# Retention decay moved from x into q, with the opening and the last tile of a fused retention + MLP kernel reordered

## The chip, the cores and the metric

The kernel runs on one core of a Trainium2 chip. The core has five engines that run at the same time, each through its own list of instructions in order: TensorE (PE, matrix products; its weight loads are shown apart as PEld), VectorE (DVE), ScalarE (ACT), GpSimd (POOL) and SyncE (SP). They wait for each other through semaphores. Sixteen DMA engines move data between the main memory and the core's SBUF; SP, ACT and POOL issue the transfers. TensorE writes to eight banks of PSUM, and only DVE and ACT read them in this kernel.

The metric is the device time of one execution in microseconds, lower is better. Three runs of the kernel before took 316.67, 316.84 and 317.51 us; the median is 316.84.

## What is computed

Eight batches of retention (attention without softmax, with a decay by distance), and after it an MLP over all 4608 tokens with the activation h * cos(h):

```python
def _attn_ref(q, k, v) -> np.ndarray:      # 8 batches, 8 heads, 576 positions, 64 wide
    B, H, S, D_ = q.shape
    scale = 1.0 / np.sqrt(D_)
    scores = scale * np.matmul(q, k.transpose(0, 1, 3, 2))
    gamma = 1.0 - 2.0 ** (-5.0 - np.arange(H, dtype=np.float32))
    pos = np.arange(S)
    rel = pos[:, None] - pos[None, :]
    Dmat = np.where(rel >= 0, gamma[:, None, None] ** rel[None, :, :], 0.0)
    ret = scores * Dmat[None, :, :, :]
    return np.matmul(ret, v).astype(np.float32)

def _moe_ref(x, w_in, w_out) -> np.ndarray:   # w_in 512 x 2048, w_out 2048 x 512
    h = x @ w_in
    g = h * np.cos(h)
    return (g @ w_out).astype(np.float32)
```

The decay gamma^(i-j) is split into two factors: gamma^i / 8 belongs to the query's position (the 8 is the scale), gamma^-j to that of k and v. So a causal mask of zeros and ones is all that the scores need, and a running state (the sum of k times v over the chunks so far) carries what earlier chunks give.

## The kernel before

**Retention.** A batch has 576 positions, cut into four chunks of 128 and one of 64 (`ck_of`). For a chunk r the steps are:
- k is cast to bf16 into `kqb` (`cast`, L314), v is multiplied by gamma^-j into `vb` (`vmul`, L305), both on POOL.
- k and q are needed with the head dimension on the partitions, in `kqt`. Batches 2 to 7 are turned by a DMA transpose (`prep`, L321). Batches 0 and 1 are turned on TensorE against the identity: `turn_k` (L352), and `turn_q` (L369), which turns a pair of heads for all positions; an eviction on ACT or DVE copies the PSUM bank into `kqt`. Batch 0's q is loaded in four pieces (`load_q0`) and cast by DVE (`cast_q0`, L278).
- `scores` (L405) multiplies q and k for the eight heads, and DVE applies the causal mask (`mk`) into `rt`, in two instructions.
- `rest` (L433) multiplies the state `sb` by q and `rt` by vb into one bank, adds the chunk's part to the state bank `st`, copies it into `sb` with two ACT instructions, and multiplies the result by `up` (gamma^i / 8) on DVE into `xt` (L476). `xt` is the MLP's input, x turned.

`up` is made by four exponentials on ACT in the opening (`consts_b`, L243), gamma^-j (`wv`) by eight small ones.

**MLP.** Nine blocks of 512 tokens. `mlp1` (L489) makes 128 of the 2048 hidden columns: four matmuls, the cosine on ACT (as a sine, `cb`), the product on DVE (`gt`). `mlp2` (L514) makes a quarter of a tile of 128 output tokens: four matmuls against `wout`; after the fourth quarter ACT copies the bank into `osb` and a store is issued by ACT. Block 0 goes through its 16 steps quarter by quarter over the four tiles (step n is tile n % 4, quarter n // 4), so step 4 first needs the second quarter of w_out, step 8 the third, step 12 the fourth. Later blocks go tile by tile. The retention of batch j+1 is put in between the steps of block j by hand.

**The order is written out by hand** in `emit` (L550). Each engine does its work in the order in which it is emitted there, and so do the queues of SP and POOL. What bears on the change:
- SP loads k0, the four pieces of q, then v0, k1, v1, k2, k3, v2, v3, k4, v4 of batch 0, without waits. After it come the ten loads of k and v of batch 1, whose first waits for w_out's first quarter (`after=[w]`).
- POOL makes the casts and multiplies of batch 0, and between them issues the loads of w_in in five pieces (hidden tiles 0-1, 2-3, 4-7, 8-11, 12-15, `WI`), after the ones of chunk 4 those of w_out in four pieces, with q of batch 1 (`load_qx`) after the second. These transfers convert from float32 to bf16 on the way.
- TensorE turns and processes chunks 0 to 3 of batch 0, with `spin` (products of the identity with itself, whose results nobody reads) in the pauses. Then the 16 steps of `mlp1` of block 0 with chunk 4's turn, scores and rest after steps 2, 4 and 6; then the 16 steps of `mlp2` of block 0, with batch 1's turns, scores and rest after steps 7 to 14. The turn of batch 1's chunk 2 uses the bank `po`, as `rest` does.
- Between `exp` and the sine ACT loads another table (L604), in the list after the eviction of k3's turn.
- The last output tile is made like any other: 16 matmuls of 512 columns, one copy, one store.

## Time and profile before

| what | us |
|---|---|
| profiled execution, whole | 316.4 |
| its span | 314.7 |
| median of three runs | 316.84 |
| TensorE busy | 303.5 |
| DVE busy | 174.1 |
| ACT busy | 162.3 |
| POOL busy | 93.1 |
| multiply into `xt`, 128x512, on DVE, 31 times | 0.69 each |
| cast of k or q, 128x512, on POOL, 56 times | 0.61 each |
| multiply of v, 128x512, on POOL, 32 times | 1.04 each |
| cast of q, 128x576, on DVE, 4 times | 0.46 each |
| eviction of a turned q, 128x576: ACT / DVE | 0.65 / 0.75 |
| cast or eviction of k's turn, 128x512: ACT / DVE | 0.59 / 0.68 |

The profile is that of one execution; the times of all runs scatter around it, so it is read by its own span, and the 1.7 us between span and time are what lies around the program. Busy shares are averages: in the opening, up to about 20 us, TensorE waits for loads and for other engines; from there on it is nearly always at work. The page's strips over 40 slices of the span show the same, with the rate of the DMA engines under them:

```profile
PE   6989999999999999999999999999999999999996
POOL 2692027535454434453445424210000000000000
DMA  7999999999999999999999999940001100120021
```

Each digit is a slice of 7.9 us, in tenths. The DMA engines are busy without a pause from the second slice to the 26th.

### The profile page before, as it was taken

To read this page: it belongs to the slowest core of one execution; us is meant where nothing else is said; L and a number is where in the kernel's file an instruction comes from. 1 tells how busy PE (TensorE), PEld (TensorE's weight loads), DVE (VectorE), ACT (ScalarE), POOL (GpSimd) and SP (SyncE) were. 2 spreads that over 40 slices of the span, in tenths; PEclk is the share of its full clock that TensorE was granted. 3 is DMA by queue.
4 is the path that set the end of the run, shared out by engine and by line. 5 is a ranking of instruction groups with operands and counts; after the bars stand their busy time and mean duration, and the time that the engine had idled before them with its cause. 6 is when DMAs were issued, how large, how long until landed. Compare 5 with 4: busy or idle time off the path is not lost.

```text
span 314.7 us, 6424 instructions
## 1 busy us (share of the span) xinstructions
PE 303.5 (96%) x2516; PEld 159.6 (51%) x2552; DVE 174.1 (55%) x301; ACT 162.3 (52%) x290; POOL 93.1 (30%) x128
## 2 busy tenths in 40 slices
PE   6989999999999999999999999999999999999996
PEld 5754455666544455445544554455444544444442
DVE  3567624787527743685458644765387438405700
ACT  7566525785337533763277236723473257316711
POOL 2692027535454434453445424210000000000000
PEclk9999999999999999999999999999999999999999
DMA  7999999999999999999999999940001100120021
GB/s 218 213 168 204 203 220 247 264 192 209 212 256 183 217 210 247 217 224 217 259 208 202 225 204 221 172 85 35 33 0 38 66 33 0 42 94 1 12 83 74
DMA packets 142814, 48.85 MB, mean 155 GB/s; under 512 B 132544, under 2 KB 137664, under 8 KB 142784
## 3 DMA queue, kind: packets, MB, share of 16 engines
q1 hardware_dynamic: 132320, 34.22, 59.7%
q0 software_dynamic: 5280, 4.78, 9.5%
q10 hardware_dynamic: 5184, 9.44, 8.9%
q8 instruction: 20, 0.33, 0.4%
q14 instruction: 10, 0.08, 0.1%
HBM read 36.70 MB, written 9.44 MB: 147 GB/s over the span
## 4 chain that ended last, share of the span: by engine, by line
PE 90%; DMA 2%; DVE 2%; ACT 2%; issue 2%; SPq 1%; POOL 0%; DVEq 0%
PE mm L401 59%; PE mm L403 20%; PE po L401 6%; PE sc L401 4%; DMA kn<-in_k_dram 2%; PE st L401 1%; DVE gt L507 1%; DVE rt L428 1%; SPq L276 1%; ACT sb L471 0%; DVE xt L476 0%; ACT L604 0%; ACT osb L538 0%; ACT kqt L365 0%; SPq L267 0%
## 5 line engine op out<-in xcount | busy, mean ns | idle before, releaser
L507 DVE TENSOR_TENSOR gt<-mm,cb 128x512 bf16<-128x512 f32 (+2 forms) x160 | 101.1, 637 | 66.2 <-ACT cb L504 63.6
L401 PE MATMUL mm<-xt,win 128*128 128x512 bf16 (+2 forms) x468 | 116.0, 358 | 1.0 <-DVE xt L476 0.3
L504 ACT ACTIVATE cb<-mm,c_pih 128x512 bf16<-128x512 f32 (+2 forms) x160 | 101.9, 645 | 27.8 <-PE mm L403 27.0
L401 PE MATMUL mm<-wout,gt 128*128 128x512 bf16 x408 | 111.8, 380 | 2.3 <-issue 1.7
L401 PEld LDWEIGHTS mm<-xt,win 128*128 128x128 bf16 x480 | 44.6, 98 | 48.8 <-DVE gt L507 2.3
L401 PEld LDWEIGHTS mm<-wout,gt 128*128 128x128 bf16 x432 | 39.3, 98 | 45.1
L403 PE MATMUL mm<-xt,win 128*128 128x512 bf16 (+2 forms) x160 | 57.2, 358 | 0.3
L538 ACT ACTIVATE osb<-mm 128x512 f32<-128x512 f32 x36 | 21.5, 597 | 68.0 <-PE mm L403 68.0
L403 PE MATMUL mm<-wout,gt 128*128 128x512 bf16 x144 | 54.6, 379 | 0.5
L308 POOL TENSOR_TENSOR vb<-vn,wv 128x512 bf16<-128x512 f32 (+1 forms) x40 | 41.7, 1043 | 29.2 <-DMA vn<-in_v_dram 24.7
L428 DVE TENSOR_TENSOR rt<-sc,mk 128x512 bf16<-128x512 f32 (+1 forms) x78 | 45.8, 625 | 4.8 <-PE sc L403 4.8
L476 DVE TENSOR_TENSOR xt<-po,up 128x512 bf16<-128x512 f32 (+1 forms) x39 | 24.7, 634 | 41.9 <-PE po L403 41.8
L471 ACT ACTIVATE sb<-st 64x256 bf16<-64x256 f32 x64 | 24.2, 378 | 40.1 <-PE st L403 38.7
L318 POOL CAST kqb<-kn 128x512 bf16<-128x512 f32 (+1 forms) x40 | 24.4, 611 | 65.2 <-DMA kn<-in_k_dram 56.2
L318 POOL CAST kqb<-qn 128x512 bf16<-128x512 f32 (+1 forms) x30 | 18.5, 615 | 17.7 <-DMA qn<-in_q_dram 17.5
L403 PEld LDWEIGHTS mm<-xt,win 128*128 128x128 bf16 x160 | 15.7, 98 | 15.7
L403 PEld LDWEIGHTS mm<-wout,gt 128*128 128x128 bf16 x144 | 14.1, 98 | 17.0
L401 PE MATMUL po<-rt,vb 128*64 128x128 bf16 (+1 forms) x273 | 15.2, 220 | 0.0
L401 PE MATMUL sc<-kqt 64*128 64x128 bf16 (+1 forms) x273 | 14.7, 215 | 0.0
L401 PEld LDWEIGHTS po<-kqt,sb 128*128 128x128 bf16 x124 | 8.6, 98 | 7.8 <-DVE rt L428 1.6
L401 PEld LDWEIGHTS po<-rt,vb 128*64 128x64 bf16 (+1 forms) x273 | 9.3, 108 | 5.9 <-DVE rt L428 2.1
L401 PE MATMUL po<-kqt,sb 128*128 128x128 bf16 (+1 forms) x124 | 11.2, 213 | 0.4 <-DVE rt L428 0.2
(88 smaller groups left out, 133.2 us busy)
## 6 DMA issues: line engine op xcount, KB each, us to landing
out_dram<-osb ACTq DMA_DIRECT2D x36, 256.0 KB, 3.3
kn<-in_k_dram SPq DMA_DIRECT2D x32, 256.0 KB, 4.7
vn<-in_v_dram SPq DMA_DIRECT2D x32, 256.0 KB, 5.3
qn<-in_q_dram SPq DMA_DIRECT2D x24, 256.0 KB, 4.8
wout<-in_moe_w_out_dram POOLq DMA_DIRECT2D x4, 512.0 KB, 14.5
win<-in_moe_w_in_dram POOLq DMA_DIRECT2D x3, 512.0 KB, 8.2
qn<-in_q_dram SPq DMA_DIRECT2D x4, 288.0 KB, 4.7
kn<-in_k_dram SPq DMA_DIRECT2D x8, 128.0 KB, 3.5
```

Source lines behind the costliest of these rows:

```text
L276: s.dma("sp", f"q0_{c}", lambda e: e.dma_start(dst, src), writes=[self.bQN[c]])
L308: self.s.op(eng, lambda e: e.tensor_tensor(bass.AP(self.VB[i][r], 0, v3), self.staged("v", r, v3[1:]), bass.AP(self.WV, r * H_, [[NCH * H_ ...
L318: self.s.op(eng, lambda e: e.tensor_copy(o, f), reads=[self.bST32[x][r]], writes=[bt[i][r]])
L401: self.nc.tensor.matmul(o, a, b, **kw)
L403: return s.done("pe", self.nc.tensor.matmul(o, a, b, **kw), reads, writes)
L428: self.s.op("dve", lambda e: e.tensor_tensor(bass.AP(self.RT[k][hp], 0, p3), bass.AP(sc[0], 0, p3), bass.AP(self.MK, 0, [[CH, ck], [0, NP] ...
L471: s.op("act", lambda e: e.activation(bass.AP(self.SB[r % 2], 64 * hp * 512 + 64 * hp, [[512, 64], [128, NP], [1, D_]]), bass.AP(self.ST, 6 ...
L476: s.op("dve", lambda e: e.tensor_tensor(bass.AP(self.XT, t0, [[NP * XR, 128], [XR, NP], [1, ck]]), bass.AP(po, 0, [[512, 128], [CH, NP], [ ...
L504: s.op("act", lambda e: e.activation(co, mo, AF.Sin, bias=self.C_PIH.ap(), scale=1.0), reads=[bm, self.bC], writes=[bcb])
L507: s.op("dve", lambda e: e.tensor_tensor(bass.AP(g, dt * TB + o, [[16 * TB, 128], [1, n]]), mo, co, ALU.mult), reads=[bm, bcb], writes=[bg])
L538: s.op("act", lambda e: e.activation(o.ap(), m.ap(), AF.Copy), reads=[bm], writes=[bo])
```

## The change

- **Decay.** `xt` becomes a plain copy. q is multiplied by gamma^i / 8 instead: for batches 0 and 1 in `turn_q`'s eviction, now always on DVE, and for the others on POOL in `qmul`, which replaces the cast of q and uses a new small table `upn` made by eight exponentials on ACT (`consts_n`).
- **Batch 0's casts.** q's casts move from DVE to POOL; k3's cast moves from POOL to ACT. The copies into `xt` of chunks 1 and 2 go to ACT, and scores and rest of chunks 1 and 3 use other banks.
- **Loads.** k1 comes before v0 and k2 before v1. k4 and v4 wait for the first piece of w_in, the loads of batch 1 for the last one. w_in has four equal pieces. The first is issued after v1's multiply, the other three after v3's.
- **Order.** Chunk 4 of batch 0 moves from after steps 2, 4, 6 to after steps 6, 8, 10 of `mlp1`. Batch 1's turns, scores and rest in `mlp2` of block 0 move by one step or two, and the turn of chunk 2 takes another bank. The sine's table load comes after chunk 2's rest.
- **Last tile.** The new function `last` makes it in two halves of 256 columns; DVE and ACT copy one each, SP and ACT store one each.

```diff
-WI = (0, 2, 4, 8, 12, 16)
+WI = (0, 4, 8, 12, 16)
...
+    def consts_n(self):
+        s = self.s
+        for h in range(H_):
+            s.op("act", lambda e: e.activation(
+                bass.AP(self.UPN, h, [[NCH * H_, 128], [H_, NCH]]), self.IP.ap(), AF.Exp,
+                bias=self.C_LN8.ap(), scale=self.lng[h]), reads=[self.bIP, self.bC], writes=[Buf()])
+        self.bUPN.w = [Tok("act", "act", s.count["act"], {})]
...
     def cast_q0(self, c):
         n = 9 * D_
-        self.s.op("dve", lambda e: e.tensor_copy(
+        self.s.op("pool", lambda e: e.tensor_copy(
...
+    def qmul(self, eng, b, r):
+        i = b % 2
+        self.mul(eng, "q", r, self.KQB[i][r], DM, 2 * DM, self.UPN, self.bUPN, self.bQB[i][r])
+
+    def mul(self, eng, x, r, t, o, pitch, w, bw, bt):
+        ck = ck_of(r)
+        self.s.op(eng, lambda e: e.tensor_tensor(
+            bass.AP(t, o, [[pitch, ck], [D_, H_], [1, D_]]),
+            self.staged(x, r, [[D_, H_], [1, D_]]),
+            bass.AP(w, r * H_, [[NCH * H_, ck], [1, H_], [0, D_]]), ALU.mult),
+            reads=[self.bST32[x][r], bw], writes=[bt])
...
     def prep(self, b, r):
-        for x in "kq":
-            self.cast("pool", x, b, r)
+        self.cast("pool", b, r)
+        self.qmul("pool", b, r)
         self.vmul("pool", b, r)
...
-        fn = (lambda e: e.activation(o, f, AF.Copy)) if eng == "act" else (lambda e: e.tensor_copy(o, f))
-        done = s.op(eng, fn, reads=[bm], writes=[Buf()])
+        u = bass.AP(self.UP, c * S_, [[NP * S_, 128], [9, 64], [1, 9]])
+        done = s.op("dve", lambda e: e.tensor_tensor(o, f, u, ALU.mult), reads=[bm, self.bUP],
+                    writes=[Buf()])
...
-        s.op("dve", lambda e: e.tensor_tensor(
-            bass.AP(self.XT, t0, [[NP * XR, 128], [XR, NP], [1, ck]]),
-            bass.AP(po, 0, [[512, 128], [CH, NP], [1, ck]]),
-            bass.AP(self.UP, q0, [[NP * S_, 128], [S_, NP], [1, ck]]), ALU.mult),
-            reads=[bpo, self.bUP], writes=self.bXT[t0 // GR:(t0 + ck) // GR])
+        o = bass.AP(self.XT, t0, [[NP * XR, 128], [XR, NP], [1, ck]])
+        f = bass.AP(po, 0, [[512, 128], [CH, NP], [1, ck]])
+        fn = (lambda e: e.activation(o, f, AF.Copy)) if eng == "act" else (lambda e: e.tensor_copy(o, f))
+        s.op(eng, fn, reads=[bpo], writes=self.bXT[t0 // GR:(t0 + ck) // GR])
...
+    def last(self, j, st):
+        s, g, n = self.s, self.GT[j % 2], DM // 2
+        i = self.n_osb % self.NOSB
+        for half in range(2):
+            m, bm = self.bank()
+            self.group([(m[:, 0:n],
+                         bass.AP(g, c * TB + 128 * st, [[16 * TB, 128], [1, 128]]),
+                         bass.AP(self.WOUT, c * DM + n * half, [[16 * DM, 128], [1, n]]),
+                         dict(start=c == 0, stop=c == 15)) for c in range(16)],
+                       self.bGT[j % 2] + self.bWOUT, [bm])
+            o, f = self.OSB[i][:, n * half:n * half + n], m[:, 0:n]
+            b = Buf()
+            b.w, b.r = list(self.bOSB[i].w), list(self.bOSB[i].r)
+            if half:
+                s.op("act", lambda e: e.activation(o, f, AF.Copy), reads=[bm], writes=[b])
+            else:
+                s.op("dve", lambda e: e.tensor_copy(o, f), reads=[bm], writes=[b])
+            dst = bass.AP(self.out, (TB * j + 128 * st) * DM + n * half, [[DM, 128], [1, n]])
+            s.dma(("sp", "act")[half], f"o_{half}", lambda e: e.dma_start(dst, o), reads=[b])
```

The order in `emit`, new lines only (the old order is that described above):

```python
        self.load("k", 0, 0)
        self.load_q0()
        for x, r in (("k", 1), ("v", 0), ("k", 2), ("v", 1), ("k", 3), ("v", 2), ("v", 3)):
            self.load(x, 0, r)
        self.consts_a()
        for c in range(NP):
            self.consts_b(c)
        self.consts_n()
        self.cast("pool", 0, 0)
        for c in range(NP):
            self.cast_q0(c)
        self.cast("pool", 0, 1)
        self.vmul("pool", 0, 0)
        self.cast("pool", 0, 2)
        self.vmul("pool", 0, 1)
        w = [self.w_in_load(0)]
        for r in (2, 3):
            self.vmul("pool", 0, r)
        for i in (1, 2, 3):
            w.append(self.w_in_load(i))
        for x in "kv":
            self.load(x, 0, 4, after=w[:1])
        self.casts(0, 4)
        for i in range(NWO):
            self.w_out_load(i)
            if i == 1:
                self.load_qx(1)
        po, st = (self.PO, self.bPO), (self.ST, self.bST)
        self.spin(30, po)
        self.turn_k(0, 0, st, "dve")
        for c in range(NP):
            self.turn_q(0, c)
            self.spin((8, 5, 5, 16)[c], po)
        self.scores(0, 0)
        self.turn_k(0, 1)
        self.spin(10, po)
        self.scores(0, 1, sc=[self.bank(), self.bank()])
        self.spin(8, po)
        self.turn_k(0, 2)
        self.rest(0, 0)
        self.scores(0, 2)
        self.cast("act", 0, 3)
        self.spin(6)
        self.rest(0, 1, self.bank(), "act")
        self.turn_k(0, 3, eng="dve")
        self.spin(8)
        self.scores(0, 3, sc=[self.bank(), self.bank()])
        self.rest(0, 2, eng="act")
        s.op("act", lambda e: e.activation(self.JUNK.ap(), self.C_PIH.ap(), AF.Sin), reads=[self.bC])
        self.spin(12)
        self.rest(0, 3, self.bank())
        self.spin(8, po)
        for r in range(NCH):
            for x in "kv":
                self.load(x, 1, r, after=w[3:])
        for r in range(NCH):
            self.casts(1, r)
```

And in the two stages after it:

```diff
         for dt in range(16):
             self.mlp1(0, dt)
-            if dt == 2:
+            if dt == 6:
                 self.turn_k(0, 4)
-            if dt == 4:
+            if dt == 8:
                 self.scores(0, 4)
-            if dt == 6:
+            if dt == 10:
                 self.rest(0, 4)
...
-                    self.turn_q(1, c, ("act", "dve")[c % 2], spare[c])
-            if n in (8, 10):
-                self.turn_k(1, n // 2 - 4, spare[0])
-            if n in (9, 12):
-                self.scores(1, n // 3 - 3)
-            if n == 13:
+                    self.turn_q(1, c, spare[c])
+            if n in (9, 11):
+                self.turn_k(1, n // 11, spare[0])
+            if n in (10, 13):
+                self.scores(1, n // 13)
+            if n == 14:
                 self.rest(1, 0)
-            if n == 14:
-                self.turn_k(1, 2, spare[0])
+                self.turn_k(1, 2, self.bank())
...
-                self.mlp2(j, n // 4, n % 4)
+                if (j, n // 4) != (NTB - 1, 3):
+                    self.mlp2(j, n // 4, n % 4)
         self.flush()
+        self.last(NTB - 1, TB // 128 - 1)
```

## The prediction, made before the changed kernel ran

> **What bounds the kernel now.** I read the page first: the span, the share of each engine, and the chain that ended last.
>
> ```profile
> span 314.7 us, 6424 instructions
> PE 303.5 (96%) x2516; PEld 159.6 (51%) x2552; DVE 174.1 (55%) x301; ACT 162.3 (52%) x290; POOL 93.1 (30%) x128
> PE 90%; DMA 2%; DVE 2%; ACT 2%; issue 2%; SPq 1%; POOL 0%; DVEq 0%
> ```
>
> TensorE sets the time. A multiply taken off DVE is worth nothing by itself; what counts is when TensorE is made to wait. So next I read TensorE's rows in order of time, around the places that the diff touches (start, length, instruction, and in brackets the idle time before).
>
> ```profile
> 19.11 0.38 PE L401 MATMUL mm<-kqt,sb 128*128 128x128 bf16 x4 [0.62 <-ACT sb L471]
> 20.86 0.59 PE L401 MATMUL mm<-xt,win 128*128 128x512 bf16 x2 [0.34 <-DVE xt L476]
> 36.16 0.81 PE L401 MATMUL mm<-wout,gt 128*128 128x512 bf16 x3
> 44.64 0.59 PE L401 MATMUL mm<-wout,gt 128*128 128x512 bf16 x2 [0.16 <-POOL kqb L318]
> 53.70 0.40 PE L401 MATMUL po<-kqt,sb 128*128 128x128 bf16 x4
> 312.32 0.34 ACTq L545 DMA_DIRECT2D out_dram<-osb  x1
> ```
>
> The first MLP matmul starts at 20.86, the second product of token block 0 at 36.16, its step n=8 (the first to need the third quarter of w_out) at 44.64. From 20.86 to 311.7 TensorE hardly stops. Then the DMA side of the opening, which the chain hardly shows: POOL's rows, and the two DMA queues in two stretches (packets, MB, share).
>
> ```profile
> 20.43 0.63 POOL L318 CAST kqb<-kn 64x512 bf16<-64x512 f32 x1
> 21.01 1.06 POOL L308 TENSOR_TENSOR vb<-vn,wv 64x512 bf16<-64x512 f32 x1
> 22.00 1.54 POOL L303 DMA_DIRECT2D wout<-in_moe_w_out_dram  x2
> 23.54 0.75 POOL L290 DMA_DIRECT2D qx<-in_q_dram  x1
> 24.27 1.50 POOL L303 DMA_DIRECT2D wout<-in_moe_w_out_dram  x2
> ```
>
> From 29 to 36 us, where only POOL's queue moves data:
>
> ```profile
> q0 software_dynamic: 1375, 1.43, 121.8%
> q1 hardware_dynamic: 18, 0.00, 0.5%
> ```
>
> From 37 to 42 us, with SP's loads of batch 1 beside it:
>
> ```profile
> q0 software_dynamic: 771, 0.77, 90.8%
> q1 hardware_dynamic: 769, 0.20, 29.8%
> ```
>
> Alone, the weights stream at 1.43/7 = 0.204 MB/us. Beside k and v loads the two queues alternate packet by packet (771 against 769), so the weights fall to 0.77/5 = 0.154 MB/us and k and v crawl at 154 packets/us. The opening is a race between that stream and TensorE. The third w_out quarter shows the margin (its issue, then the time to its landing):
>
> ```profile
> L303 POOL DMA_DIRECT2D wout<-in_moe_w_out_dram x1: 762/762/762, 24.3 to 24.3; - x1
> DMA to landing us min/median/max: 17.1/17.1/17.1
> ```
>
> It lands at 41.4 and is needed at 44.64: 3.3 us to spare. The q tile for batch 1 lands at 23.5 + 14.5 = 38.0, the second quarter at 34.7.
>
> **The change part by part.**
>
> *x copied plainly, q multiplied instead.* The multiply into xt takes 691 ns for 128x512; a DVE cast of that shape out of PSUM takes 684 (the kt eviction): 0.007 x 39, off the path, nothing. On POOL the q cast (615 ns) becomes a multiply like v's (1044): 0.43 x 30 = 13 us more on an engine with 56 us of waits for k loads alone. TensorE waits for no transposed tile in this profile. If that cover went, one late q tile would cost 0.4. The eight extra exponentials cost ACT 0.9 us at 6 to 7 us, where it idles. In batch 1 all four q turns are evicted by DVE (about 0.75 each, 3.0 in a row, from 43.6); scores now come a step later, so nothing waits.
>
> *The opening.* A q cast on POOL takes about 0.69 (0.611 x 576/512) instead of 0.46 on DVE, so the scores of chunk 0 start about 0.25 later. k1 comes before v0, so chunk 1 is cast at 9.4 instead of 10.6. The Sin table load (1.28 us) sits in the chain before chunk 3's state eviction; row 19.11 shows its 0.62 of waiting. It moves behind chunk 2's copies. Hop by hop: k2 lands at 12.3 (when the load of that place in the queue landed before), its cast ends 12.9 (0.61), its turn and ACT eviction 14.0 (0.45 and 0.60), chunk 0's two state evictions 14.8 (0.78), k3's cast on ACT 15.4 (taken as 0.60, like an eviction of that shape), its turn and DVE eviction 16.6 (0.45 and 0.68); chunk 3's scores follow, its two masks run from 17.1 to 18.4 (1.29), its last products start at 18.45 and its xt runs from 19.2 to 19.9 (0.69), instead of 20.6. The first w_in piece is issued at 14.3 (after v1's multiply) and lands near 19.6: 2.3 to first bytes (issued at 13.86, the old one had 4 packets by 16.2), 0.524/0.204 = 2.6, 0.4 of ramp and tail. So MLP could start 0.65 earlier (bounds 0 and 0.9).
>
> *The loads of k4 and v4, and what queues behind them.* They now wait for the first w_in piece. On POOL, their cast and multiply stand before the five issues of w_out and qx; before, these issues began at 22.0, deep in the w_in stream, so the queue never ran dry. Now:
> 1. SP issues k4 and v4 at 19.6. First packets: 1.0 later at best (the first load of all, 256 KB, took 3.2 from issue to landing), 3.7 at worst (batch 1's loads, issued at 32.2, show 18 packets by 36). They have 2 x 512 packets; at 154/us that is 6.6. v4 lands between 27.2 and 29.4 (w_in is done near 29, and then they have the DMA to themselves); I take 28.8, since the congested start is the like case.
> 2. v4's multiply (1.06), then w_out is issued at 29.8, its first bytes 2.3 later: 32.1 (30.5 to 32.7). The stream stood empty from 29 on.
> 3. Batch 1's loads are released by the last w_in piece (29.5) instead of w_out's first quarter (32.2), so they run beside w_out from its first byte. Three quarters and qx are 3 x 0.524 + 0.590 = 2.16 MB; at 0.154 that is 14.0. The third quarter lands at 46.3 (44.7 to 46.9).
> 4. With its lead of 0.65, TensorE would be at n=8 near 44.0. It waits for 46.3 and starts 1.7 after the old 44.64 (0.1 to 2.3). qx lands near 42.9, so the turns of q wait a little too, inside the same gap. The last quarter (49.7) comes before n=12.
>
> [...]
>
> *After n=8.* The turns of batch 1 have the same work one or two steps later. The turn of chunk 2 no longer uses the po bank: row 53.70 came 0.25 after the matmuls before it would have let it, behind that eviction. I take -0.2 (0 to -0.25).
>
> *Last tile in halves.* The final eviction falls from 597 ns to that of 128x256 on ACT (376): -0.22. The store takes 2.3 from its issue to the end of the span; with half the bytes between -0 and -1.2; I take -0.25, a fifth of the far end: halving a load here (256 to 128 KB of k) moves the median landing from 4.7 to 3.5 in a crowded queue, and this one is alone. 32 matmuls of 256 columns cost what 16 of 512 do. Together -0.47 (-0.2 to -1.4).
>
> *Sum.* +1.7 - 0.2 - 0.47 = +1.0 (-1.5 to +2.1). The profiled execution took 316.4 (span 314.7 and 1.7 around it): 317.4. The median of the runs shown lies 0.4 above it: 317.8.
>
> **The rivals.**
>
> *B, the stream is in time: faster.* If v4 lands by about 26.5 (or w_out moves at nearly the lone rate), the third quarter lands by 44.0 and the opening's lead stays: -0.65 - 0.2 - 0.47 = -1.3, 315.5. For it: the margin was 3.3, k4 and v4 are only 0.26 MB, and w_out's issue could reach its first bytes sooner than w_in's 2.3. Against it: the packet-by-packet rows, and batch 1's first k load, also 1024 packets, which took 11.6 from issue to landing.
>
> *C, the gap costs more than itself: slower still.* From 42.3 to 46.3 TensorE would do only the turns of q. In the opening, 29 idle-time matmuls against the identity took 2.88 us (99 ns each) after a pause, later 15 took 0.84 (56). If TensorE returns to the slow pace for as long, the price is 29 x 43 ns = 1.25: 319.1. Against it: the granted clock reads 1.00 in every stretch, the opening's included, and waits up to 0.6 did no such thing. [...]
> [...]
>
> *D, the change doesn't do what it says in the opening.* If the xt chain is not shortened, the start is as before; with the stall the sum stays, since the stall hides the lead, and in case B 0.65 is lost: 316.2, no change.
>
> **How the numbers follow.** About 0.3% (0.95 us) is what can be told from no change. The forecast 0.55, with its own range 316.3 to 318.5 (the stall's two ends, the other terms as taken), about half of it above 317.8; B 0.25; C 0.12; D 0.08. Slower: 0.28 + 0.12 + 0.04 = 0.44. Same: 0.24 + 0.04 + 0.02 = 0.30. Faster: 0.03 + 0.21 + 0.02 = 0.26. The range 315.3 to 319.3 leaves out about a tenth at each end.
>
> **What would show it.** Right: POOL's first w_out issue near 30 instead of 22, q0 empty between 29 and 32, TensorE waiting 1 to 3 us for a w_out matmul near 44 with nothing on POOL, DVE or ACT in front. Wrong: w_out issued before 27, or no wait at n=8; then the start of the first MLP matmul (20.2 or 20.9) tells B from D. C shows as matmuls of 128x512 slower than 379 ns after the gap. The tail shows as the time from the last matmul to the end of the span: 3.0 before, 2.5 after.

## The result, and the profile after

The changed kernel takes 321.40 us (median of four runs, 321.25 to 321.51); the kernel before, run beside it, 317.13 (four runs, 316.67 to 317.51). The ratio is 1.0135, with a 95% interval of 1.0118 to 1.0153. The forecast was 317.8, its range 315.3 to 319.3: the kernel is slower, as the likeliest case had it, but by four times as much, and outside the range.

The page of the changed kernel, from an execution of 321.33 us: the span, the engines, and the chain that ended last by engine.

```profile
span 319.6 us, 6480 instructions
PE 303.3 (95%) x2530; PEld 161.4 (51%) x2566; DVE 176.6 (55%) x303; ACT 161.1 (50%) x294; POOL 106.8 (33%) x130
PE 81%; DMA 11%; SPq 2%; issue 2%; POOL 2%; DVE 1%; ACT 0%
```

TensorE's busy time is what it was (303.5 before), in a span that is 4.9 longer. DMA has 11% of the chain, where it had 2%. So TensorE does the same work and waits more. TensorE's rows in order of time (start, length, instruction, and in brackets the idle time before it and what ended it) show where:

```profile
20.62 0.59 PE L424 MATMUL mm<-xt,win 128*128 128x512 bf16 x2 [0.34 <-DVE xt L501]
29.82 0.24 PE L424 MATMUL mm<-ident,kqb 64*128 64x64 bf16 x3 [3.21 <-POOL kqb L339]
38.94 0.81 PE L424 MATMUL mm<-wout,gt 128*128 128x512 bf16 x3
49.70 0.59 PE L424 MATMUL mm<-wout,gt 128*128 128x512 bf16 x2 [2.15 <-DMA wout<-in_moe_w_out_dram]
60.03 0.58 PE L424 MATMUL mm<-xt,win 128*128 128x320 bf16 x3
63.85 0.57 PE L424 MATMUL mm<-xt,win 128*128 128x320 bf16 x3 [0.27 <-DVE gt L529]
```

Two long waits stand in block 0: 3.21 for the cast of k4 (chunk 4's turn), and 2.15 for the third quarter of w_out (step n=8). The same places in both kernels:

| place on TensorE | before | after | shift |
|---|---|---|---|
| first MLP matmul | 20.86 | 20.62 | -0.24 |
| block 0, second product starts | 36.16 | 38.94 | +2.78 |
| step n=8 | 44.64 | 49.70 | +5.06 |
| block 1, first MLP matmul | 55.23 | 60.03 | +4.80 |
| block 1, second product starts | 74.88 | 80.28 | +5.40 |
| block 2, first MLP matmul, and every later stage | 92.68 | 98.08 | +5.40 |
| end of the span | 314.7 | 319.6 | +4.9 |

So n=8 is 5.06 late, 0.26 is won behind it, 0.60 is lost in block 1's first stage, and the tail gives back 0.5. The sum is 4.9. POOL's rows say why w_out came late:

```profile
29.07 0.60 POOL L339 CAST kqb<-kn 64x512 bf16<-64x512 f32 x1 [9.55 <-DMA kn<-in_k_dram]
29.69 1.03 POOL L328 TENSOR_TENSOR vb<-vn,wv 64x512 bf16<-64x512 f32 x1
30.68 1.54 POOL L314 DMA_DIRECT2D wout<-in_moe_w_out_dram  x2
32.22 0.75 POOL L301 DMA_DIRECT2D qx<-in_q_dram  x1
32.95 1.50 POOL L314 DMA_DIRECT2D wout<-in_moe_w_out_dram  x2
```

POOL stood 9.55 us for k4, with the five issues behind it, which began at 22.00 before and begin at 30.68 now. The chain of waits up to n=8 is one line from the first piece of w_in to that matmul (start, length, what; pieces of under 0.06 named "issue" are left out):

```profile
14.23 5.87 DMA win<-in_moe_w_in_dram
20.12 8.90 DMA kn<-in_k_dram
29.07 0.60 POOL kqb L339
29.69 1.03 POOL vb L328
30.72 1.50 POOL wout L314 x2
32.23 0.72 POOL qx L301
32.95 16.48 DMA wout<-in_moe_w_out_dram
49.43 0.27 issue
49.70 0.59 PE mm L424 x2
```

Three stretches of the two DMA queues explain its two long pieces (packets, MB, share of 16 engines). From 20.9 to 24.5, with k4 and v4 already issued by SP (q1):

```profile
q0 software_dynamic: 717, 0.72, 120.6%
q1 hardware_dynamic: 2, 0.00, 0.1%
```

From 30.7 to 33.5, with w_out already issued by POOL (q0):

```profile
q1 hardware_dynamic: 2443, 0.62, 102.8%
...
q0 software_dynamic: 2, 0.00, 0.4%
```

From 36 to 50:

```profile
q0 software_dynamic: 2132, 2.18, 94.0%
q1 hardware_dynamic: 1884, 0.48, 25.7%
```

In the first, k4 and v4 move 2 packets in 3.6 us, while w_in moves 717. In the second the picture is reversed: w_out moves 2, while batch 1's loads, which the last w_in piece released, move 2443. In the third, w_out, with qx, runs at 2.18/14 = 0.156 MB/us.

The tail, from the rows of the last tile:

```profile
315.39 0.42 DVE L581 COPY osb<-mm 128x256 f32<-128x256 f32 x1 [10.63 <-PE mm L426]
317.14 0.38 ACT L579 ACTIVATE osb<-mm 128x256 f32<-128x256 f32 x1 [2.90 <-PE mm L426]
317.55 0.34 ACTq L583 DMA_DIRECT2D out_dram<-osb  x1
```

From the start of the last copy to the end of the span it is 319.6 - 317.14 = 2.46. Before, it was 314.66 - 311.70 = 2.96:

```profile
311.70 0.60 ACT L538 ACTIVATE osb<-mm 128x512 f32<-128x512 f32 x1 [2.86 <-PE mm L403]
```

The 32 matmuls of 256 columns take nearly what the 16 of 512 took: from the last tile's first matmul to the last copy it is 317.14 - 313.45 = 3.69, and was 311.70 - 308.05 = 3.65.

### The profile page after: what moved, and what is told of

Read it like the earlier page. It is cut to its first block, busy times and chain, and to the rows that moved or that the text cites. A ratio compares the mean times of both kernels' runs of the same rounds, so it can differ in the third digit from the quotient of the medians.

```text
span 319.6 us, 6480 instructions
## 1 busy us (share of the span) xinstructions
PE 303.3 (95%) x2530; PEld 161.4 (51%) x2566; DVE 176.6 (55%) x303; ACT 161.1 (50%) x294; POOL 106.8 (33%) x130
## 4 chain that ended last, share of the span: by engine, by line
PE 81%; DMA 11%; SPq 2%; issue 2%; POOL 2%; DVE 1%; ACT 0%
PE mm L424 53%; PE mm L426 18%; PE po L424 5%; DMA wout<-in_moe_w_out_dram 5%; PE sc L424 3%; DMA kn<-in_k_dram 3%; DMA win<-in_moe_w_in_dram 2%; DMA vn<-in_v_dram 2%; SPq L278 2%; PE st L424 1%; DVE gt L529 1%; POOL vb L328 1%; SPq L287 1%; POOL wout L314 0%; POOL qx L301 0%
## 5 line engine op out<-in xcount | busy, mean ns | idle before, releaser
L424 PE MATMUL mm<-wout,gt 128*128 128x512 bf16 (+1 forms) x426 | 112.1, 372 | 4.3 <-DMA wout<-in_moe_w_out_dram 2.1
L424 PEld LDWEIGHTS mm<-wout,gt 128*128 128x128 bf16 x450 | 41.0, 98 | 46.9 <-DMA wout<-in_moe_w_out_dram 2.6
L426 PE MATMUL mm<-wout,gt 128*128 128x512 bf16 (+1 forms) x142 | 53.6, 378 | 0.5
L560 ACT ACTIVATE osb<-mm 128x512 f32<-128x512 f32 x35 | 20.9, 597 | 64.4 <-PE mm L426 64.4
L451 DVE TENSOR_TENSOR rt<-sc,mk 128x512 bf16<-128x512 f32 (+1 forms) x76 | 44.5, 623 | 5.9 <-PE sc L426 5.9
L501 DVE CAST xt<-po 128x512 bf16<-128x512 f32 (+1 forms) x37 | 23.3, 630 | 39.1 <-PE po L426 39.0
L328 POOL TENSOR_TENSOR kqb<-qn,upn 128x512 bf16<-128x512 f32 (+1 forms) x30 | 31.3, 1042 | 16.5 <-DMA qn<-in_q_dram 16.1
L426 PEld LDWEIGHTS mm<-wout,gt 128*128 128x128 bf16 x142 | 13.9, 98 | 16.5
## 6 DMA issues: line engine op xcount, KB each, us to landing
wout<-in_moe_w_out_dram POOLq DMA_DIRECT2D x4, 512.0 KB, 13.8
```

Of the source, the lines that this page charges most:

```text
L328: self.s.op(eng, lambda e: e.tensor_tensor(bass.AP(t, o, [[pitch, ck], [D_, H_], [1, D_]]), self.staged(x, r, [[D_, H_], [1, D_]]), bass.A ...
L424: self.nc.tensor.matmul(o, a, b, **kw)
L426: return s.done("pe", self.nc.tensor.matmul(o, a, b, **kw), reads, writes)
L451: self.s.op("dve", lambda e: e.tensor_tensor(bass.AP(self.RT[k][hp], 0, p3), bass.AP(sc[0], 0, p3), bass.AP(self.MK, 0, [[CH, ck], [0, NP] ...
L501: fn = (lambda e: e.activation(o, f, AF.Copy)) if eng == "act" else (lambda e: e.tensor_copy(o, f))
L560: s.op("act", lambda e: e.activation(o.ap(), m.ap(), AF.Copy), reads=[bm], writes=[bo])
```

## The experiments

All twelve, in three groups. "Before beside it" is the kernel before, run on the same chip in the same session; its median lay between 317.05 and 317.37 in the four sessions (17 to 29 runs each, on three chips), so versions of different sessions are compared by their ratios. Diffs are against the changed kernel unless another base is named.

| run | median us (runs) | ratio to before, 95% interval |
|---|---|---|
| w_out issued ahead of chunk 4's cast | 320.38 (5) | 1.009 [1.0053, 1.0127] |
| batch 1's loads after w_out's first quarter | 321.15 (4) | 1.0133 [1.0095, 1.0172] |
| k4, v4 loaded without a wait | 317.69 (10) | 1.0013 [0.9989, 1.0036] |
| before, with k4, v4 waiting for w_in | 325.66 (4) | 1.0273 [1.024, 1.0306] |
| w_out first, wait filled with work | 319.29 (6) | 1.007 [1.0048, 1.0091] |
| w_out first, chunk 4 four steps later | 316.50 (12) | 0.9978 [0.9962, 0.9994] |
| that, with batch 1's old steps | 317.54 (12) | 1.0014 [0.9998, 1.0029] |
| that, with the old bank for one turn | 317.36 (12) | 1.0004 [0.9991, 1.0017] |
| before, with the decay in q | 317.12 (10) | 0.9997 [0.9979, 1.0015] |
| chunk 4 later, five memsets on DVE | 316.12 (11) | 0.9975 [0.9965, 0.9984] |
| before, with 49 memsets on DVE | 316.86 (10) | 0.9997 [0.9983, 1.0011] |
| before, with the last tile in halves | 316.60 (12) | 0.998 [0.9961, 0.9999] |

### The wait for k4 and what queues behind it

**w_out issued ahead of chunk 4's cast.**

```diff
         for x in "kv":
             self.load(x, 0, 4, after=w[:1])
-        self.casts(0, 4)
         for i in range(NWO):
             self.w_out_load(i)
             if i == 1:
                 self.load_qx(1)
+        self.casts(0, 4)
```

> The changed kernel, with POOL's issues of w_out and of batch 1's q moved ahead of the cast and multiply of chunk 4; k4 and v4 still wait for the first w_in piece. Theory S (the weight stream stands empty because w_out's issue is queued behind v4): the stream runs on at 28, the third w_out quarter lands near 43 and TensorE no longer waits at n=8 (2.15 us in the changed kernel). TensorE still waits some 3 us for k4 at step 6. Time 319.0 (318.5 to 319.6). Rival T (w_out is late because batch 1's loads share the DMA engines from the start): the third quarter stays near 49, the time above 320.5.

The wait at n=8 is gone, that for k4 remains, in TensorE's rows of this kernel:

```profile
29.68 0.24 PE L424 MATMUL mm<-ident,kqb 64*128 64x64 bf16 x3 [2.78 <-POOL kqb L339]
47.23 0.59 PE L424 MATMUL mm<-wout,gt 128*128 128x512 bf16 x2 [0.16 <-issue]
```

So the waits came out as theory S has them; the third quarter lands at 43.4. The profiled run took 318.83, 2.5 less than the changed kernel's; in that pair this is the worth of POOL's order alone. The other four took 319.90 to 321.60, and the median of 320.38 lies above the expected 318.5 to 319.6: see the filled wait below.

**Batch 1's loads held back.**

```diff
         for i in range(NWO):
-            self.w_out_load(i)
+            wo = self.w_out_load(i)
+            if i == 0:
+                w.append(wo)
...
-                self.load(x, 1, r, after=w[3:])
+                self.load(x, 1, r, after=w[4:])
```

> The changed kernel, with batch 1's loads waiting for w_out's first quarter, as before, instead of w_in's last piece; k4, v4 and POOL's order stay as changed. If the sharing has a part in it: first bytes of w_out 2.3 us after its issue instead of 3.2, the lone rate up to about 39 us, third quarter near 45.3, no wait at n=8, and the wait for k4 is left: 319.2 (318.7 to 319.8). If the pause of the stream alone decides (S without T): third quarter after 48, 320.3 or more.

TensorE's rows here:

```profile
47.30 0.59 PE L424 MATMUL mm<-wout,gt 128*128 128x512 bf16 x2 [0.16 <-issue]
53.54 0.34 PE L424 MATMUL po<-ident,kqb 128*128 128x128 bf16 x3 [2.04 <-POOL kqb L339]
```

Step n=8 no longer waits and starts 2.4 earlier than in the changed kernel: the third quarter, issued at 32.99, lands 13.8 later, at 46.8. So batch 1's loads had a part in its delay. But the turn of batch 1's k1 now waits 2.04, and block 1 begins at 59.98 instead of 60.03. The time is that of the changed kernel, above the 318.7 to 319.8 that was expected for a part of the sharing: batch 1's loads, held back for w_out, were themselves needed a few us later. Sharing the DMA time differently did not win back here what was lost while k4 was awaited.

**k4 and v4 loaded without a wait.**

```diff
-        for x, r in (("k", 1), ("v", 0), ("k", 2), ("v", 1), ("k", 3), ("v", 2), ("v", 3)):
+        for x, r in (("k", 1), ("v", 0), ("k", 2), ("v", 1), ("k", 3), ("v", 2), ("v", 3),
+                     ("k", 4), ("v", 4)):
             self.load(x, 0, r)
...
-        for x in "kv":
-            self.load(x, 0, 4, after=w[:1])
```

> The changed kernel, with k4 and v4 loaded right after v3 without a wait, as before; POOL's order stays as changed. Theory S: both waits (3.2 us for k4 at step 6, 2.15 us for w_out at n=8) go, since v4 is there long before POOL comes to it; w_out is issued near 22. The first w_in piece lands about 1 us later, as k4 and v4 share with it. Time 317.3 (316.3 to 317.9). Rival T (batch 1's loads, released by w_in's end, are what costs): w_out's third quarter is still too late for n=8, time above 318.5.

Both long waits are gone, and the time is that of the kernel before. A smaller wait comes in their place: the two loads now share the DMA engines with the first w_in piece (from 17 to 20, 297 of SP's packets run beside 440 of w_in's), for which TensorE waits 1.10, and the first MLP matmul starts at 22.53. Its row and that of n=8:

```profile
22.53 0.59 PE L424 MATMUL mm<-xt,win 128*128 128x512 bf16 x2 [1.10 <-DMA win<-in_moe_w_in_dram]
46.01 0.59 PE L424 MATMUL mm<-wout,gt 128*128 128x512 bf16 x2 [0.16 <-issue]
```

So holding k4 and v4 back did buy what it was meant for; it cost more than it bought.

**The kernel before, with that one wait added.**

```diff
-                     ("v", 2), ("v", 3),
-                     ("k", 4), ("v", 4)):
+                     ("v", 2), ("v", 3)):
             self.load(x, 0, r)
...
-        self.w_in_load(1)
+        w1 = self.w_in_load(1)
+        for x in "kv":
+            self.load(x, 0, 4, after=[w1])
```

> The kernel before, with one thing of the change: k4 and v4 wait for w_in's second piece (the same 0.52 MB as the changed kernel's first). Theory: that wait alone makes the loss. k4 lands near 30, TensorE waits some 6 us for it at step 2 of the first product, w_out is issued near 32 instead of 22; time 321.5 to 324. Rival (it takes the other moves as well): within 1 us of the kernel before.

The wait alone makes the kernel before slower, by 2.7%, more than expected. Chunk 4 is turned after step 2 there, so TensorE waits longer. One row, and the windows around it (stretch, length, busy time of PE, PEld, DVE, ACT and POOL, granted clock, DMA share, GB/s):

```profile
31.61 0.34 PE L401 MATMUL mm<-ident,kqb 64*128 64x64 bf16 x3 [7.51 <-POOL kqb L318]
31.93 0.61 PE L401 MATMUL mm<-xt,win 128*128 128x512 bf16 x1
```

```profile
28.00:32.00 4.00, 0.39 (x5) 0.30 (x6) 0.00 (x0) 0.00 (x0) 0.74 (x2) 0.50 0.69 119
32.00:36.00 4.00, 4.00 (x17) 1.39 (x18) 0.69 (x1) 1.51 (x3) 4.00 (x6) 0.50 0.36 30
36.00:40.00 4.00, 4.00 (x27) 1.85 (x26) 2.90 (x6) 1.95 (x4) 0.62 (x1) 0.87 1.11 171
40.00:44.00 4.00, 4.00 (x20) 1.77 (x19) 3.01 (x6) 3.12 (x6) 0.00 (x0) 1.00 1.20 199
```

The granted clock falls to 0.50 in the pause and stays there for some 5.4 us of full work (0.50 from 36 to 37, 0.97 from 37 to 38); a matmul of 128x512 that takes 0.38 elsewhere takes 0.61. Block 0's second product starts 10.2 late: the MLP began 0.5 later than in the profile of the kernel before, the pause is 7.5, and the 2.2 left is an estimate of what the clock of 0.50 cost. This is rival C, at a longer pause than the change has. In the profiled run with w_out first, whose pause was 2.78, the clock read 1.000, and in the changed kernel's it read 1.00 through one of 3.21.

**w_out first, and TensorE kept at work in the wait.**

```diff
             if dt == 6:
+                self.spin(48, po)
                 self.turn_k(0, 4)
```

The base is the run with w_out first. The added products are those of the identity with itself.

> This is the version with w_out's issues ahead of chunk 4's cast and multiply (320.38, five runs from 318.83 at clock 1.0 to 321.6 at 0.989), with 48 products of the identity with itself (48 x 56 ns = 2.7 us) put where TensorE waits 2.78 for k4, so that it is at work instead of idle. The length of the wait is the same. Theory: the 2.8 us without work make the granted clock fall in most runs, and that costs 1 to 3 us more than the wait. Then all runs stay near the profiled 318.8, the median is 318.6 to 319.2, the lowest and highest lie within 0.8, and the clock reads 1.0 in each. Rival: the scatter has another origin (the arrival of the first loads); then the median stays at 320.0 to 320.6 and the scatter at 2 to 3 us. If the wait has become shorter by then than the added work, the time is up to 0.5 higher in both cases.

| | runs, us | mean granted clock |
|---|---|---|
| w_out first | 318.83; 319.90, 320.38, 320.46; 321.60 | 1.000; 0.995 three times; 0.989 |
| the same, wait filled | 318.69 to 319.95 (six) | 1.000 in all |

The median falls by 1.1 to 319.29 (0.1 above what was expected, and the spread of 1.3 is wider than the 0.8 expected), and no run shows a lower clock. The two profiled runs differ by 0.2 only, 318.83 and 319.02, so the profile of the unfilled one, taken at full clock, doesn't show what its other runs lost: 1 to 3 us, more where the clock was lower. That the pause is what lowers the clock in them is likely and not shown. The two versions ran on different chips, and their ratios to the kernel before, 1.009 and 1.007, have intervals that overlap; the kernel before, which has no such pause, also shows 0.995 in 2 of the 24 runs beside the unfilled version, the two longest (318.82 and 319.48); and no pause of an unprofiled run is on record. One thing is mixed in: the filled version gains 0.24 between block 1's first MLP matmul and block 2's (37.79 against 38.03), a matter that the next group takes up.

**w_out first, and chunk 4 four steps later.**

```diff
-            if dt == 6:
+            if dt == 10:
                 self.turn_k(0, 4)
-            if dt == 8:
+            if dt == 12:
                 self.scores(0, 4)
-            if dt == 10:
+            if dt == 14:
                 self.rest(0, 4)
```

> As e1_wout_first (w_out issued ahead of chunk 4's cast), and chunk 4 of batch 0 four steps later in the first product: after steps 10, 12 and 14 instead of 6, 8 and 10. If the two waits were all that the change lost in the opening: no wait of TensorE for k4 (cast near 29, needed near 30.5) nor for w_out; the second product starts near 36.0, step n=8 near 44.5, and with the 0.5 of the last tile and the 0.35 that was lost after n=8 the time is 316.5 (315.8 to 317.2). If the late k4 also drags the stream or batch 1 behind it: 318 or more.

No wait for k4 or w_out is left; the longest between 20 and 52 us is 0.44, for k1 of batch 1. Block 1 begins at 55.37, where the changed kernel had 60.03 and the kernel before 55.23:

```profile
48.93 0.34 PE L424 MATMUL po<-ident,kqb 128*128 128x128 bf16 x3 [0.44 <-POOL kqb L339]
55.37 0.58 PE L424 MATMUL mm<-xt,win 128*128 128x320 bf16 x3
```

With both waits gone the kernel is a little faster than the one before (0.2%, the interval just clear of none), though the 0.6 of block 1 is still in it. So the two waits were the loss.

### The 0.6 in block 1's first stage

From block 1's first MLP matmul to block 2's it is 92.68 - 55.23 = 37.45 before, and 98.08 - 60.03 = 38.05 after, with no transfer waited for. Three parts of the change were tried, and then the place of one instruction.

**Batch 1's old steps**, on the version with chunk 4 later (the turn of chunk 2 keeps its new bank):

```diff
-            if n in (9, 11):
-                self.turn_k(1, n // 11, spare[0])
-            if n in (10, 13):
-                self.scores(1, n // 13)
-            if n == 14:
+            if n in (8, 10):
+                self.turn_k(1, n // 2 - 4, spare[0])
+            if n in (9, 12):
+                self.scores(1, n // 3 - 3)
+            if n == 13:
                 self.rest(1, 0)
+            if n == 14:
                 self.turn_k(1, 2, self.bank())
```

> As e5_chunk4_later, with batch 1's turns, scores and first rest back at the steps of the kernel before (turns after n=8, 10, 14, scores after 9, 12, rest after 13); the turn of chunk 2 keeps a bank of its own. Theory: the move to n=14 lost 0.6 in block 1's first stage (from 60.0 to 80.3 in the changed kernel, 20.25, against 19.65 before) and won 0.25 at the bank; with the old steps 0.6 comes back: 315.9. Rival: that 0.6 came from batch 1's late loads: no difference to e5_chunk4_later, or a new wait for k1 at n=10.

The stretch is 38.06: not the order of the steps. The median of 317.54 fits neither expectation, though. It is 1.0 above that of the version with chunk 4 later, in the same session; the profiled run began its MLP 1.45 later (22.17 against 20.72), with a granted clock of 0.91 up to 20 us, but ten of the twelve runs show a clock of 1.000. The edit touches nothing so early, and why the opening differs isn't shown. So this group is read by the stretch in the trace and not by medians.

**The kernel before, with the decay in q**: `qmul`, `consts_n`, `turn_q` and the plain copy into `xt` as in the change, q's casts of batch 0 on POOL, all exponentials ahead, all else as before.

> The kernel before, with the decay moved into q and nothing else but what that needs: turned q of batches 0 and 1 evicted by DVE with the multiply, q of the others multiplied on POOL, x copied on DVE, q's casts of batch 0 on POOL, all exponentials ahead. The opening's scores start about 0.25 to 0.5 later, nothing else changes: 317.5 (317.1 to 318.0). Rival: 13 us more of POOL work shows later on as a wait for turned tiles: above 318.

The stretch is 37.45 and the time that of the kernel before: not the decay.

**The old bank for the turn of chunk 2**, on the version with chunk 4 later:

```diff
-                self.turn_k(1, 2, self.bank())
+                self.turn_k(1, 2, spare[0])
```

> This is the version with chunk 4 four steps later (316.50, span 314.9), with one thing put back: the turn of batch 1's chunk 2 uses the po bank again, as in the kernel before. Theory: taking a bank from MLP's rotation of four at that place is what costs the 0.6 us in block 1's first stage, because the four tiles of block 0 hold all four banks until their copies, so each of the first hidden tiles gets its bank one copy later. Then the time from the first MLP matmul of block 1 to its first mlp2 matmul falls from 20.25 (after) to 19.65 as in the kernel before, 0.26 of it is given back in front (the turn waits for the po copy again), and the kernel takes 316.1 to 316.3. Rival: the bank is not the cause (the order of the steps and the decay were already found not to be); then the stage stays 0.6 longer and the time is 316.5 to 316.8.

The stretch is 38.04, so it is not the bank: the theory fell. (The median of 317.36, at a ratio of 1.0004, is again above what either expectation gave; this profile's MLP starts at 21.67.) What did show was that the filled wait above, which touches nothing here, had lost a part of the delay, and that in every version with the 0.6 it begins at one instruction. In the rows of ACT and DVE of the changed kernel:

```profile
60.79 1.07 ACT L526 ACTIVATE cb<-mm,c_pih 128x320 bf16<-128x320 f32 x2 [0.17 <-PE mm L426]
```

```profile
61.82 0.89 DVE L529 TENSOR_TENSOR gt<-mm,cb 128x320 bf16<-128x320 f32 x2 [1.85 <-PE sc L426]
```

The same two in the kernel before:

```profile
55.99 1.07 ACT L504 ACTIVATE cb<-mm,c_pih 128x320 bf16<-128x320 f32 x2 [0.49 <-PE mm L403]
56.62 1.03 DVE L507 TENSOR_TENSOR gt<-mm,cb 128x320 bf16<-128x320 f32 x2 [1.44 <-ACT cb L504]
```

In the changed kernel the first cosine of block 1 runs from 60.79 to 61.32, and the multiply that needs it starts at 61.82, although its matmul ended before the cosine began. The releaser named, the scores, is not one that it waits for. Counted from 0, semaphore waits included, this multiply is entry 63 of DVE's list in the changed kernel and in all versions with a stretch of 38.03 to 38.06, but 78 in the kernel before, 75 with the decay alone and 68 in the filled one, whose added group brings five more waits. Counted from block 1's first MLP matmul, it is 0.40 later than in the kernel before; the next seventeen multiplies are 0.2 to 0.4 later, and in the stage of 192 columns, where DVE's rows stand one behind the other, that grows to 0.60. Why it grows there isn't shown.

**Five memsets on DVE**, on the version with chunk 4 later:

```diff
+        for y in range(5):
+            s.op("dve", lambda e: e.memset(self.DUM[:, y:y + 1], 0.0))
         for dt in range(16):
             self.mlp1(0, dt)
```

> The version with chunk 4 four steps later (316.50, span 314.9), with five one-column memsets added to DVE's list ahead of block 0's first hidden tile; nothing reads them, and DVE's next work waits for TensorE there. Theory: in every trace so far a multiply into gt whose place in DVE's own list (waits counted, from 0) is 63, 127, 191 and so on starts 0.40 to 0.45 late with nothing to wait for; in the changed kernel and all versions of it that is the first multiply of block 1 (place 63), where DVE has no slack, and in the kernel before it is not (place 78). With five more it has place 68. Then the row of that multiply follows its cosine at once (0.63 after the cosine's start instead of 1.03), the time from the first MLP matmul of block 1 to the one of block 2 falls from 38.05 to 37.45, and the kernel takes 315.8 to 316.2. Rival: the place is chance; then the multiply is late as before, the stretch stays 38.05, and the time is 316.4 to 317.3.

The same two rows in this kernel:

```profile
56.07 1.07 ACT L527 ACTIVATE cb<-mm,c_pih 128x320 bf16<-128x320 f32 x2 [0.17 <-PE mm L427]
```

```profile
56.70 1.03 DVE L530 TENSOR_TENSOR gt<-mm,cb 128x320 bf16<-128x320 f32 x2 [1.44 <-ACT cb L527]
```

The multiply follows its cosine by 0.63 instead of 1.03, the stretch is 92.76 - 55.32 = 37.44, and 316.12 is the best time of all. Five instructions whose results nobody reads took the 0.6 away.

**The kernel before, with 49 memsets on DVE**, which move that multiply to entry 127:

```diff
         for n in range(16):
+            for y in range(49 if n == 2 else 0):
+                s.op("dve", lambda e: e.memset(self.DUM[:, y:y + 1], 0.0))
             self.mlp2(0, n % 4, n // 4)
```

> The kernel before, with 49 one-column memsets added to DVE's list after block 0's last multiply into gt, in 6 us where DVE idles; nothing reads them. They move the first multiply of block 1 from place 78 to place 127 of DVE's list. Theory (each 64th place of the list costs DVE 0.4): that multiply now starts 1.03 instead of 0.63 after its cosine, the stretch from block 1's first MLP matmul to block 2's grows from 37.45 to 38.05, and the kernel takes 0.6 more than the kernel before beside it (317.1): 317.5 to 317.9. Rival: the delay belongs to something else in the changed kernel; then the stretch stays 37.45 and the time is that of the kernel before within 0.2.

This expectation failed: at entry 127 the multiply is on time (57.01, its cosine at 56.38). The expectation had every 64th entry; the traces hold every 128th. Over the 14 traces a multiply into `gt`, behind its own wait, stood 25 times at entry 63, 191, 319 or 447, and started 0.39 to 0.46 after that wait's end each time; 15 times it stood at 127, 255 or 383, and started 0.05 after it each time. Of all the other multiplies behind a wait, some two thousand, none starts more than 0.3 after it with DVE idle. (With the decay alone, entry 63 is a multiply of block 0 at 38.5, where DVE has slack.) The mask multiplies that stand at entry 191 or 447 directly behind another one, ten in all, start as soon as that one ends, so an instruction that is still at work covers the gap. In this kernel entry 191 is the twenty-ninth multiply of block 1, deep in the stage of 192 columns, and DVE's row there shows a gap after a cosine, where the kernel before has fourteen multiplies in one row:

```profile
74.47 1.27 DVE L508 TENSOR_TENSOR gt<-mm,cb 128x192 bf16<-128x192 f32 x4 [0.34 <-ACT cb L505]
```

The stretch is 0.26 longer than before (37.71), but that isn't shown to be this gap: the multiply ahead of it, the twenty-eighth, is 0.26 later already, and the filled wait, whose list has no such place there, has 0.34 (37.79). So in these traces the place in the list decides whether a multiply is late, in steps of 128; in the versions with entry 63 it explains the 0.6, and the smaller 0.26 and 0.34 stay open.

### The last tile

**The kernel before, with the last tile in halves**: `last` and its call as in the change, nothing else.

> The kernel before, with the last output tile in two halves and nothing else changed. From the last eviction's start to the end of the span 2.5 us instead of 3.0: 0.5 less than the kernel before (0.3 to 0.6). Rival: the store's time is fixed, only the shorter copy tells: 0.2 less.

From the last copy's start to the end of the span it is 2.45 in this trace, as expected, against 2.96. The median is 0.63 below the 317.23 of the kernel before beside it, with an interval that just leaves out no change. The tail is the part of the change that pays.

## Why the prediction was right and wrong

**Right in kind.** It forecast slower, by w_out's third quarter being late behind k4 and v4 on POOL. The trace shows that line link by link, and undoing POOL's order or the wait takes the stall at n=8 away. That the sign came out is no luck, then; the size and the range were missed. The shares of the sum, from the two profiled executions:

| term | predicted | measured |
|---|---|---|
| start of step n=8 | +1.7 (0.1 to 2.3) | +5.06 |
| after n=8 (po bank) | -0.2 | -0.26 |
| block 1's first stage | nothing | +0.60 |
| last tile | -0.47 | -0.50 |
| sum | +1.0 | +4.9 |

**The step that failed** is the section "The loads of k4 and v4, and what queues behind them", steps 1 to 3: the third quarter was put at 46.3 (44.7 to 46.9) and landed at 49.43. The 3.1 between them come in three parts, each a size of a term and not its direction.

- Step 1: k4 was issued at 20.12, not 19.6, since the first w_in piece took 5.87 and not 5.3 from its issue. Its first packets took longer than the "3.7 at worst": from 20.9 to 24.5, that is up to 4.4 after its issue began, two had moved. Then they went faster than at 154/us (620 in the next 3.7 us). Together, w_out was issued at 30.7 instead of 29.8: 0.9.
- Step 2: its first bytes were put 2.3 after the issue, by the row of w_in. But in 30.7 to 33.5 q0 moved 2 packets, the first of them 2.7 after the issue: 0.4 more. Batch 1's loads, 2443 packets in that stretch, stood in front: with them held back (the second experiment) q0 had moved 13 packets by 32.5, 1.8 after the same issue.
- Step 3: the rate was right (0.156 against 0.154 MB/us), the amount was not. The third quarter should need 2.16 MB from the first bytes on. But q0's trace also has packets of 4 bytes, sixteen for each transfer (144 for nine), and those that close the third quarter run from 46.77 to 49.11: its slowest part ends 2.3 after its fastest. By the last of them q0 had moved 2.37 MB, of which 0.21 is the fourth quarter's: 0.21/0.156 = 1.3. The landing is 0.3 later still. The first 2.5 us went slower (0.32 MB from 33.5 to 36), which is about 0.4. From first bytes to landing it is 16.1, where the step has 14.0 in its sum and 14.2 in its result: 32.1 and 14.0 make 46.1, and no term stands for the 0.2 up to 46.3.

Together that is 0.9 + 0.4 + 1.9 = 3.2, the 3.1 but for rounding.

**What was not charged at all** is TensorE's own wait for k4. The cast of k4 was counted for POOL's queue, but `turn_k(0, 4)` after step 6 needs it too. The prediction's own numbers, with the measured place, bound it: TensorE reaches it at 29.82 - 3.21 = 26.6; k4, the first half of the packets, would have landed between 25.5 (28.8 less half of 6.6) and 28.8, and its cast ended 0.6 later: a wait of 0 to 2.8. In the changed kernel it hides in the larger stall at n=8, which is set by a landing and not by TensorE. But it is what is left when the order on POOL is mended (2.78), and a price in clock seems to come on top (in four of five runs a clock of 0.989 to 0.995, and 1 to 3 us).

**The opening.** The lead was put at 0.65 (0 to 0.9) and is 0.24. The chain to `xt` ended at 20.34 instead of 19.9, most of it lost at the last products (18.86 instead of 18.45). It made no difference, as the prediction said, because the stall hides it. What the new opening is worth without the stall isn't shown: with k4 and v4 behind the first w_in piece and the changed opening, the first MLP matmul starts between 20.62 and 22.17 in eight traces, five of them at or below 20.76; with the old opening it starts at 20.86, 21.14 and 21.65 in three. (A missing record of one matmul can shift such a start by 0.2: the page of the changed kernel has 468 records of these matmuls for 480 of their weight loads, and one starts 0.22 after another.)

**Block 1's first stage.** The sum has no term for it. The 0.60 comes from the place of one multiply in DVE's list, which no row of the profile before shows as a cost.

**The decay.** Right: nothing. POOL's busy time grew from 93.1 to 106.8, against 13 more foreseen, and by itself the edit leaves the time at a ratio of 0.9997.

**The rivals.** B (the stream in time) fell: w_out's issue was at 30.7, not before 27. C (the gap costs more than itself) did not happen in the profiled run, whose clock reads 1.00 through pauses of 3.21 and 2.15. Two of the changed kernel's four runs show 0.995, and take 0.2 more, so C is not the miss. But it is real: the clock fell to 0.50 in a pause of 7.5 us. With w_out first, where the profiled pause was 2.8, four of five runs had a lower clock and took 1 to 3 us more; that the pause did it isn't shown. At what length of a pause the clock falls isn't shown: it read 1.00 through 3.21 in one trace and fell in a pause of 7.51 in another. D can't be told: the one pair of profiles shows the opening shorter, by a third of what was said, which is less than the scatter above.

**The best version** takes w_out's issues ahead of chunk 4's cast, chunk 4 four steps later, and the five memsets: 316.12 against 317.08 beside it. Of the 0.96, its profile shows 0.4 in the span (314.3 against 314.7), which is the tail. The rest can't be attributed: the start of the MLP scatters between 20.6 and 22.2 over the profiles (22.5 where k4 and v4 come first).

## What to carry to other kernels

When a load gets a new wait, follow everything that reads it: the engine that casts it, every issue queued behind that cast, and the engine that will stand waiting for the tile itself; then ask which of these stands last. Transfers that were issued behind another queue's backlog started late here (k4 some 4.3 us and w_out 2.7 us after the issue, against under 1.8 for w_out with batch 1's loads held back), whatever the row of an early transfer says, and the third quarter had landed only when its slowest part was in, 2.3 us after its fastest. DMA time left empty came back here as a wait for another load (2.15 for w_out became 2.04 for k1), so sharing it differently did not mend it; what did was to refill the queue earlier and to move the consumer later.

## What the runs showed that was not expected

- A pause of TensorE had a second price in one trace: in 7.51 us without work the granted clock fell to 0.50, and it took some 5.4 us of work to return. With a pause of 2.78 in the profile, four of five runs showed a mean clock of 0.989 to 0.995 and took 1 to 3 us more than the profiled one; filled with idle products, all six ran at 1.000. That the short pause is the cause is likely and not shown.
- A multiply into `gt` behind its own wait started 0.35 to 0.41 late at every 128th entry of DVE's list (63, 191, 319, 447, waits counted), in all 25 places of the 14 traces. With the decay alone, where it falls on a multiply of block 0, the time stayed at a ratio of 0.9997; the ten mask multiplies at such a place directly behind another one, still at work, started as soon as that one ended; on the first multiply of block 1 it cost 0.6. What lies behind it can be narrowed. The profile page of the changed kernel lists ten packets of a queue of the kind "instruction", 8 KB each in the trace:

```profile
q14 instruction: 10, 0.08, 0.1%
```

After each of the 25 late entries, in all 14 traces, a packet of q14 starts within 0.3 to 2.5 us; after the 15 on time that happens once. So the late entries go together with packets of that queue. That these make them late is argued, not shown. Why the step is 128 isn't shown either.
